# Rows of the last batch six schedule points later, and expert registers loaded in pairs

## The chip, the cores and the metric

The kernel runs on one NeuronCore of a Trainium2 chip. TensorE (PE, with weight loads shown apart as PEld) multiplies, VectorE (DVE) and ScalarE (ACT) work element by element, GpSimd (POOL) and SyncE (SP) mostly issue DMAs. The metric is device microseconds of one execution; lower is better. The time before is the median of three executions, 407.94 us (407.66 to 410.76).

## What is computed

Causal attention in blocks of 64 over 8 batches, 8 heads, 576 positions and head size 64, followed by a mixture of 8 experts with one expert for each token:

```python
scores = scale * q @ k.T, masked so that block_i >= block_j
attn   = softmax(scores);  x = attn @ v, laid out as rows of 512
logits = x @ w_gate                       # 8 experts
local  = sigmoid(x @ w_local)
e      = argmax(logits) if s == 0 or local < 0.5 else the expert of the row before
p      = softmax(logits)
out    = p[e] * (relu(x @ w1[e]) @ w2[e])    # 512 -> 1024 -> 512
```

There are 4,608 rows x. The expert of a row can depend on the row before it, so it is found by a scan along each batch.

## The kernel before

**Attention.** Two heads at a time make 32 steps, four to a batch. Through all of them PE is the busy engine. What the routing needs from a batch is worked into the steps of the next batches: `logits_of` and `tokens` find each row's expert, its factor and its rank among the rows of that expert; `rows_of_batch` turns a batch's result from columns into rows with PE transposes, VectorE divides them by the softmax sums, and a DMA stores them in `x_rows` in DRAM.

**Expert tiles.** Rows are then taken in tiles of 128 with one expert each. Phase 0 has 15 tiles made of rows of the first five batches; `slots_first` lists their rows. Phase 1 takes all that is left, the last batch included; `slots_second` lists its rows (`idx1`) and experts (`et1`). Twenty-three phase-1 tiles are always run, which makes 38 (tiles 0 to 37); five more stand behind a branch (L1469) that is not taken here. For a tile, GpSimd gathers its rows from `x_rows` (`gather`, L651), SyncE loads them transposed as `xT` (`rows_of`, L1388), VectorE copies the expert's first weights next to each other as `w1c` (`weights_of`, L1292), PE makes 32 products of 128 columns (`first_mm`, L1093), ScalarE applies the relu (L1096), PE makes 8 products of 512 columns (`second_mm`, L1330), ScalarE scales (L1335), and GpSimd scatters the rows to the output (L1338). In the loop the order on PE is `first_mm(i)`, `second_mm(i-1)`, `first_mm(i+1)`, and so on. `weights_of(i+1)` stands at the head of iteration i.

**Registers.** Which expert a tile has is known only on the chip. `expert` (L1102) reads the offset of its weights out of the table `et0` or `et1` in SBUF into a register on PE and into another on DVE (TENSOR_LOAD in the trace). DVE's is used by the `w1c` copy, PE's by `second_mm`.

**Work of the last batch.** When the first tiles run, the last batch is not done with. Two lists of steps remain, written as generators: `late()`, the chain that goes from the logits over `tokens` (its operations are L313 to L395) to `slots_second` (L563 to L629, and `experts_of`), and `rows()`, five steps that each turn 128 (the last 64) positions of the last batch into rows: four PE transposes (L720), one VectorE product (`x`, L767) and a DMA store. Calls of `point()` in the tile loop let them in: one after each half of `first_mm`, one before and one after `second_mm`, four to an iteration from i = 2 on, two in i = 1. At a point the chain goes first, if a credit in rough microseconds allows; where the chain takes nothing and at least `ROWS_AT` = 6 points have gone by since the last row step, a row step is let in. A chain step of kind "T" or "PE" has work for PE; a "T" step is held back until one point has gone by without work.

With the weights written in `late()`, the row steps before stand at points 7 (in `first_mm(3)`, between its halves), 13 (before `second_mm(3)`), 21 (before `second_mm(5)`), 30 (after `second_mm(7)`) and 38 (after `second_mm(9)`). The chain's transposes and products on PE stand at point 8 (`rta`, L330), 10 (`rtb`, L340), 12 (`rtd`, L350), 14 (`rtr`, L363), and 37, 42 and 44 (`rti`, L594).

**Stores and gathers.** A row step's store is held in a list and issued on SP one iteration later, behind that iteration's `rows_of` (or earlier, where `release()` is called). The first gather of phase 1, that of tile 15, is issued in iteration 12 ahead of `second_mm(11)`; before it, `release()` issues all that is still held, and the gather waits for the stores and for `idx1`. `rows_of(14)` comes on SP after that place.

Of the kernel before, what the change touches and what calls it, by code (L numbers as in the profile page):

```python
# [62 lines left out]
def kernel(  # L63
# [768 lines left out]
    with tc.tile_pool(name="atn_const", bufs=1) as cst, \  # L832
# [268 lines left out]
        def expert(ph, j, engines=(mybir.EngineType.PE, mybir.EngineType.DVE)):  # L1101
            return nc.values_load(  # L1102
                et_i[ph][0:1, j:j + 1], engines=engines, min_val=0,
                max_val=(E - 1) * WE,
                skip_runtime_bounds_check_because="the table is clamped to the last expert")
# [89 lines left out]
        for i in range(NPAIR):  # L1195
# [7 lines left out]
            if i == NPAIR - 1:  # L1203

                tiles = [(0, j) for j in range(NS[0])] + [(1, j) for j in range(NS[1])]
                ev = {j: expert(*tiles[j]) for j in range(2)}
# [79 lines left out]
    with ExitStack() as ffn:  # L1286
        f_p = ffn.enter_context(tc.tile_pool(name="ffn_s", bufs=2, reuse_waits="tile"))

        def weights_of(i):
            ev[i] = expert(*tiles[i])  # L1290
            w = f_p.tile([P, WE], BF16, tag="w1c%d" % (i % 2), name="w1c", bufs=1)
            ended["w"] = nc.vector.tensor_copy(w, w1_bf[:, bass.ds(ev[i], WE)])  # L1292
            return w

        f_p.tile([P, WE], BF16, tag="w1c1", name="w1c", bufs=1)
        f_p.tile([P, KO1, P], BF16, tag="xT0", name="xT", bufs=1)
        w_third = weights_of(2)
        for _ in range(2):
            steps.step()
# [46 lines left out]
        def late():  # L1346
            b = B - 1
            for weight, group in ((1.1, (lambda: half_batch(b, 1, gates=False),)),
                                  (1.5, (lambda: logits(b, 0), lambda: logits(b, 1)))):
                yield "PE" if weight < 1.2 else "T", weight  # L1350
                for out in [x() for x in group]:
                    out()
            yield "V", 0.4
            yield from tokens(*GROUPS[3], TS)
            yield "V", 0.8
            yield from slots_second(scratch_of([Sall.rearrange("p a h s -> p (a h s)")]))

        def rows():
            for t in range(NC):
                yield "PE", 0.7  # L1360
                if len(held) > 1:
                    release()
                rows_out(B - 1, t)()
# [9 lines left out]
            credit[0] -= spent  # L1373

        EACH, ROWS_AT = 0.6, 6
        credit, points = [0], [0]
        chain, others = Steps(late()), Steps(rows())
        def ps_x():
            return f_ps.tile([P, KO1, P], BF16, tag="rt", name="ps_x", bufs=3)
# [25 lines left out]
        more, tiles = tiles[-MORE:], tiles[:-MORE]  # L1405
# [24 lines left out]
        for i, (ph, j) in enumerate(tiles):  # L1430
            now, done = w, prev
            waiting = len(held)
            if i == 0:
                w = w_next
            elif i + 1 < len(tiles):
                w = w_third if i == 1 else weights_of(i + 1)
# [28 lines left out]
            if i == behind_tile:  # L1465

                nc.gpsimd.drain()
                n = nc.values_load(used[0:1, 0:1], min_val=0, max_val=E * BS)
                with tc.If(n > NS[1] - MORE, label="more"):  # L1469
                    more_tiles()  # L1470
        i = len(tiles) - 1
# [37 lines left out]
```

## Time and profile before

| | |
|---|---|
| median of three executions | 407.94 us |
| the profiled execution: time, span | 412.89 us, 410.8 us |
| mean granted PE clock | 0.991 |
| tile loop on PE, from `first_mm(0)` to the last product | 257.7 to 406.2 us of the span |
| DMA moved | 69.97 MB, mean 170 GB/s |

The profiled execution is 4.95 us above the median, 2.1 us of its time lie around the span, and times below are counted from the span's start. A row of the timeline gives start, length, engine, line, operation, the tiles written and read, the count of instructions merged, and in brackets how long the engine had been idle and what released it. Matmuls overlap by about 0.16 us at their ends, so a stretch is best measured from start to start.

### The profile page before, as it was taken

The page shows a single profiled execution, that of the slowest core. Times are in us where ns is not written, and L with a number is a line of the kernel's source. Part 1 is how long each engine was busy: PE and PEld are TensorE (multiplying, and loading weights), DVE is VectorE, ACT ScalarE, POOL GpSimd, SP SyncE. Part 2 cuts the span into 40 slices and gives each one's busy share as a digit, 9 for nine tenths or more (in the row PEclk, how much of TensorE's full clock was granted, in tenths as well). Part 3 has the DMA queues.
Part 4 walks back from the last instruction along what each step waited for, and adds up shares of the span by engine and source line. Part 5 has one row for each costly group of instructions (what it writes and reads, how often), then busy time and mean ns, then how long its engine had stood idle before and what let it go on. Part 6 is the DMA issues. An engine that isn't in the chain of part 4 may idle for free. (4 is left out here: it accounts for less than half of the span.)

```text
span 410.8 us, 14546 instructions
## 1 busy us (share of the span) xinstructions
PE 395.0 (96%) x5834; PEld 285.7 (70%) x5834; DVE 246.2 (60%) x505; ACT 225.7 (55%) x391; POOL 183.8 (45%) x250
## 2 busy tenths in 40 slices
PE   8999999999999999999998998979999999999985
PEld 7677777776776876776774666647777777777663
DVE  3444746646646677977999767877985333324220
ACT  4666666665765765665663654334444455445342
POOL 1325343144144054554351452246767676666603
PEclk9999999999999999999998999999999999999989
DMA  6579999998998999999978789853753544554521
GB/s 180 135 155 225 195 214 245 206 187 227 215 207 192 207 184 222 208 167 239 205 153 199 131 162 192 124 136 111 159 173 104 152 148 131 142 158 138 140 67 77
DMA packets 108819, 69.97 MB, mean 170 GB/s; under 512 B 74847, under 2 KB 100255, under 8 KB 108752
## 3 DMA queue, kind: packets, MB, share of 16 engines
q0 software_dynamic: 19200, 34.84, 40.6%
q1 hardware_dynamic: 89552, 34.19, 35.9%
q8 instruction: 48, 0.79, 0.8%
q14 instruction: 19, 0.16, 0.1%
HBM read 66.88 MB, written 14.70 MB: 199 GB/s over the span
## 5 line engine op out<-in xcount | busy, mean ns | idle before, releaser
L1019 DVE TENSOR_TENSOR S<-S,Pc 128x896 f32<-128x896 f32 (+2 forms) x96 | 86.4, 900 | 21.4 <-PE o L998 16.5
L977 PE MATMUL sc<-qkT 64*64 64x224 f32 (+6 forms) x1536 | 92.1, 369 | 0.7 <-DVE xg L818 0.7
L1292 DVE COPY w1c<-w_bf 128x4096 bf16 x36 | 44.2, 1235 | 58.5 <-PE ps_y L1330 26.1
L1096 ACT ACTIVATE hT<-ps_h 128x512 bf16<-128x512 f32 x76 | 44.1, 598 | 57.6 <-PE ps_h L1093 23.1
L1093 PEld LDWEIGHTS <-w1c 128*128 128x128 bf16 x1152 | 67.9, 98 | 10.9 <-issue 3.8
L977 PEld LDWEIGHTS sc<-qkT 64*64 64x64 f32 x1536 | 70.6, 135 | 3.2 <-DVE xg L818 1.1
L880 POOL COPY w_bf<-w_bf 128x512 f32<-128x512 f32 x61 | 42.8, 718 | 66.5 <-DMA w_bf<-in_k_dram 27.4
L1330 PE MATMUL ps_y<-w_bf,hT 128*128 x296 | 71.3, 383 | 1.0 <-issue 0.7
L1093 PE MATMUL ps_h<-xT,w1c 128*128 128x128 bf16 x1088 | 67.2, 220 | 2.6 <-ACTq L1469 2.1
L651 POOL DMA_INDIRECT xg<-x_rows,idx x38 | 49.7, 1309 | 42.2 <-issue 13.9
L987 ACT ACTIVATE Pc<-sc 128x448 f32<-128x448 f32 (+1 forms) x96 | 68.1, 716 | 0.0
L998 PE MATMUL o<-Pc,v 128*64 128x320 f32 (+2 forms) x512 | 57.6, 366 | 0.0
L1338 POOL DMA_INDIRECT out_dram<-y,idx x37 | 42.4, 1147 | 25.7 <-issue 9.5
L998 PEld LDWEIGHTS o<-Pc,v 128*64 128x64 f32 x512 | 35.0, 137 | 23.8
L987 ACT ACTIVATE S<-sc 128x576 f32<-128x576 f32 x64 | 42.0, 656 | 14.9 <-PE sc L977 14.6
L1330 PEld LDWEIGHTS <-hT 128*128 128x128 bf16 x296 | 27.7, 99 | 28.5 <-issue 3.1
L1011 ACT COPY oT<-o 128x576 f32<-128x576 f32 x32 | 20.5, 641 | 36.2 <-PE o L1007 36.2
L1335 ACT ACTIVATE y<-ps_y,xg 128x512 f32<-128x512 f32 x37 | 25.4, 687 | 20.7 <-PE ps_y L1330 17.1
L818 DVE TENSOR_TENSOR xg<-trx,rs 128x512 bf16<-128x512 f32 (+1 forms) x31 | 20.2, 684 | 26.2 <-PE trx L692 26.1
L998 PE MATMUL o<-S,v 128*64 128x320 f32 (+1 forms) x256 | 35.0, 392 | 0.3 <-ACT qkT L925 0.3
L1026 POOL MEMSET S<- 64x128 f32 x30 | 6.0, 200 | 63.2 <-DVE S L1021 22.5
L946 ACT COPY qkT<-kq 128x1024 f32<-128x1024 f32 x30 | 30.8, 1027 | 0.4 <-PE trx L692 0.4
(313 smaller groups left out, 442.3 us busy)
## 6 DMA issues: line engine op xcount, KB each, us to landing
w_bf<-in_moe_w_dram POOLq DMA_DIRECT2D x16, 1024.0 KB
w_bf<-in_k_dram SPq DMA_DIRECT2D x32, 256.0 KB
w_bf<-in_q_dram SPq DMA_DIRECT2D x32, 256.0 KB
v<-in_v_dram SPq DMA_DIRECT2D x64, 128.0 KB
x_rows<-xg POOLq DMA_DIRECT2D x24, 128.0 KB
qkl<-in_k_dram SPq DMA_DIRECT2D x32, 32.0 KB
qkl<-in_q_dram SPq DMA_DIRECT2D x32, 32.0 KB
vl<-in_v_dram SPq DMA_DIRECT2D x32, 32.0 KB
```

What stands on the lines that cost most here:

```text
L651: st = nc.gpsimd.indirect_dma_start(out=x, out_offset=None, in_=x_dram[:rows], in_offset=bass.IndirectOffsetOnAxis(ap=row_of(ph, j), axis= ...
L880: copies[j](m, raws[i][1 + j].rearrange("p h j d -> p j h d"))
L946: nc.scalar.copy(to.rearrange("p a (r s) -> p r a s", r=2), ps.rearrange("p r (a s) -> p r a s", a=2))
L977: nc.tensor.matmul(to[:, col + skip:col + n], lhsT=t[r, 0, k0:k0 + ST], rhs=t[r, 1, q0 + skip:q0 + n], start=True, stop=True)
L987: nc.scalar.activation(exps_at(i, c, q0, n, rows), ps[rows, :, col:col + n], func=AF.Exp, scale=scale_attn)
L998: nc.tensor.matmul(po[64 * h:64 * h + 64, VO + q0:VO + q0 + n], lhsT=vs[i][c][:, h, :], rhs=exps_at(i, c, q0, n, slice(0, P))[:, h, :], st ...
L1019: nc.vector.tensor_add(Ss[i][:, :, P * c:], Ss[i][:, :, P * c:], Pc[i % 2][:, :, POS[c]:POS[c] + n])
L1093: nc.tensor.matmul(ps[:, fo, :], lhsT=w[:, ko * F + f0:ko * F + f0 + P], rhs=xT[:, ko, :], start=(ko == 0), stop=(ko == KO1 - 1))
L1096: relu[0] = nc.scalar.activation(hT[:, half * (FO // 2):(half + 1) * (FO // 2), :], ps, func=AF.Relu)
L1292: ended["w"] = nc.vector.tensor_copy(w, w1_bf[:, bass.ds(ev[i], WE)])
L1330: nc.tensor.matmul(ps, lhsT=hT[:, fo, :], rhs=w2_bf[:, bass.ds(ev + fo * Dm, Dm)], start=(fo == 0), stop=(fo == FO - 1))
L1338: st = nc.gpsimd.indirect_dma_start(out=out_flat, out_offset=bass.IndirectOffsetOnAxis(ap=row_of(ph, j), axis=0), in_=y, in_offset=None, b ...
```

## The change

`weights_of(i)` loads the registers of tile i and of tile i + 1 when tile i's are not there yet, so the loads for tiles 2 and 3 stand together, then 4 and 5, and so on to 36 and 37; every second call loads nothing. The count of loads is the same. And the count of points since the last row step begins at -6 in place of 0, so the first row step waits for six points more.

```diff
         def weights_of(i):
-            ev[i] = expert(*tiles[i])
+            if i not in ev:
+                for n in range(i, min(i + 2, len(tiles))):
+                    ev[n] = expert(*tiles[n])
             w = f_p.tile([P, WE], BF16, tag="w1c%d" % (i % 2), name="w1c", bufs=1)
             ended["w"] = nc.vector.tensor_copy(w, w1_bf[:, bass.ds(ev[i], WE)])
             return w
...
         EACH, ROWS_AT = 0.6, 6
-        credit, points = [0], [0]
+        credit, points = [0], [-ROWS_AT]
         chain, others = Steps(late()), Steps(rows())
```

With the same weights, the row steps then stand at points 13, 21, 28 (after `first_mm(8)`), 35 (in `first_mm(10)`) and 43 (in `first_mm(12)`, between its halves). The chain keeps its order on each engine; a few of its steps move by one point, and `rta`, `rtb`, `rtd` and `rtr` stay where they were.

## The prediction

> **What bounds the kernel now.** I read the page's busy time by engine first, then PE's waits, and only then the timelines around the rows that the change moves.
>
> ```profile
> PE 395.0 (96%) x5834; PEld 285.7 (70%) x5834; DVE 246.2 (60%) x505; ACT 225.7 (55%) x391; POOL 183.8 (45%) x250
> ```
>
> PE is busy for 96% of the span. The PE part of the table of waits, first for 262 to 285 us, then for 282 to 388:
>
> ```profile
> PE rtb L340 <- DVE S L337: 1.3, 1, 1.3
> PE ps_y L1330 <- issue: 0.7, 2, 0.3
> ...
> PE ps_h L1093 <- issue: 0.3, 1, 0.3
> ```
>
> The columns are the sum, the count and the longest. After 282 us PE loses 0.3 us in all, so what the change does there counts only as work added to PE or as a wait that isn't there now. The one long wait before, `rtb`, is a step of the chain, and the first row step stands right ahead of it. PE's timeline there:
>
> ```profile
> 271.19 1.05 PE L1093 MATMUL ps_h<-S,w1c 128*128 128x128 bf16 x16
> 272.08 0.61 PE L720 MATMUL trx<-id_f,oT 128*128 128x128 f32 x4
> 272.52 1.06 PE L1093 MATMUL ps_h<-S,w1c 128*128 128x128 bf16 x16
> 273.93 0.27 PE L330 MATMUL rta<-id_f,S 128*5 128x128 f32 x1 [0.35 <-issue]
> 274.04 1.89 PE L1330 MATMUL ps_y<-w_bf,hT 128*128 x8
> 277.27 0.19 PE L340 MATMUL rtb<-S,ones_f 5*5 5x5 f32 x2 [1.34 <-DVE S L337]
> 277.61 1.95 PE L1093 MATMUL ps_h<-xT,w1c 128*128 128x128 bf16 x32 [0.16 <-PE rtb L340]
> ```
>
> And VectorE's in the same place:
>
> ```profile
> 268.43 1.23 DVE L1292 COPY w1c<-w_bf 128x4096 bf16 x1 [0.36 <-issue]
> 270.10 0.36 DVE L737 RECIPROCAL rs<-trl 128x32 f32<-128x32 f32 x1 [0.45 <-remote]
> ...
> 273.62 0.17 DVE L327 TENSOR_TENSOR S<-S 128x5 f32<-128x5 f32 x1
> 274.41 1.23 DVE L1292 COPY w1c<-w_bf 128x4096 bf16 x1 [0.62 <-issue]
> 275.55 0.68 DVE L767 TENSOR_TENSOR x<-trx,rs 128x512 bf16<-128x512 f32 x1
> 276.15 0.27 DVE L332 COPY S<-rta 5x128 f32<-5x128 f32 x1
> ```
>
> The reader is to see one chain: L327 ends at 273.79 and `rta` follows at 273.93; VectorE then copies `w1c`, makes row step 0's product, and only then does L332 and what follows up to L337, for which `rtb` and all of PE behind it wait. PE's four row transposes at 272.08 cost nothing here: without them `rta` would wait for L327 just as long.
>
> **The change part by part.** *(a) Row step 0 leaves this place.* On PE its 0.44 us (272.08 to 272.52) become idle time: 0. On VectorE its product goes out of the chain: 275.55 to 276.15, so `rtb` comes **0.60 us earlier**. Its store goes behind `rows_of(7)` on SP; nobody waits for that row until the gathers of phase 1.
>
> *(b) Loads in pairs.* All loads on PE, and two of them:
>
> ```profile
> L1102 PEldq TENSOR_LOAD <-et x38: 295/320/897, 249.0 to 393.8; - x38
> ...
> L1102 PEldq TENSOR_LOAD <-et x1: 300/300/300, 277.3 to 277.3; - x1
> ...
> L1102 PEldq TENSOR_LOAD <-et x1: 303/303/303, 310.5 to 310.5; - x1
> ```
>
> A load takes 0.30 us at the least, 0.32 in the middle; 38 remain. In the even part PE's own stream shows where one stands:
>
> ```profile
> 308.27 1.95 PE L1093 MATMUL ps_h<-xT,w1c 128*128 128x128 bf16 x32
> ...
> 310.25 1.89 PE L1330 MATMUL ps_y<-w_bf,hT 128*128 x8
> 311.98 1.95 PE L1093 MATMUL ps_h<-xT,w1c 128*128 128x128 bf16 x32
> ```
>
> The load at 310.5 belongs ahead of the products at 311.98: PE's sequencer is some 1.4 us early, and two loads in a row (0.6 us) fit under that; two of the longest on record (0.897, at the first tile) would stick out by 0.4. So in the even part the pairs cost and save nothing, and the eight products of 512 columns fill 310.25 to 311.98 without a gap in which a load could have cost. Without that cover a second load would cost 0.3 us and the next tile would have it back. In the chain it is another matter. The load at 277.3 stands between `rtb` and the next tile; it is tile 5's, which now comes with tile 4's: the 0.16 us wait at 277.61 goes, **-0.16**. Tile 4's call, just ahead of the `w1c` copy at 274.41, now makes two loads, on VectorE too: I take **+0.32** on the chain (between 0, if the second is hidden, and 0.62, the whole idle time that the row shows for the first). On PE the second load is ahead of the products at 271.19, and the idle time at `rta` (0.35, and 0.44 more from (a)) hides it. Tile 3's call at 268.43 makes no load: up to 0.36 less, but then L737 waits 0.45 for another reason, so I take half, **-0.18** (0 to -0.36).
>
> *(c) The row steps behind.* Steps 0 to 3 take places at or near those that steps 1 to 4 have now, so PE and VectorE do the same there. The fifth, at point 43 between the halves of the products at 308.27, is new, in a stretch in which PE never waits: **+0.44**, all of it (a lower bound would need a wait to hide it, and there is none).
>
> Sum: -0.60 - 0.16 + 0.32 - 0.18 + 0.44 = **-0.18 us**, with bounds -0.60 - 0.16 - 0.36 + 0.44 = -0.68 and -0.60 - 0.16 + 0.62 + 0.44 = +0.30. Against the profiled execution's own 412.89 us this gives 412.7; it stands 4.95 above the median of 407.94, and on that, 407.8.
>
> *(d) What the last row step sets late.* The first gather of phase 1 (tile 15) waits for every store of the last batch. Now the last is issued at 305.44, six microseconds ahead of that gather:
>
> ```profile
> 305.44 0.46 SPq L677 DMA_DIRECT2D x_rows<-x  x1
> 307.00:307.50 0.50, 0.50 (x4) 0.26 (x3) 0.50 (x2) 0.27 (x1) 0.00 (x0) 1.00 0.48 175
> 308.95 1.23 DVE L1292 COPY w1c<-w_bf 128x4096 bf16 x1 [0.27 <-issue]
> 311.60 1.38 POOL L651 DMA_INDIRECT xg<-x_rows,idx  x1 [0.56 <-DVE idx L432]
> 314.00:314.50 0.50, 0.50 (x4) 0.26 (x3) 0.50 (x1) 0.50 (x1) 0.32 (x1) 1.00 0.34 132
> L1388 SPq DMA_TRANSPOSE xT<-xg x1: 1200/1200/1200, 314.9 to 314.9; - x1
> 316.50:317.00 0.50, 0.50 (x13) 0.50 (x11) 0.00 (x0) 0.00 (x0) 0.49 (x1) 1.00 0.50 102
> 319.00 1.45 PE L1093 MATMUL ps_h<-xT,w1c 128*128 128x128 bf16 x23
> ```
>
> (The last two columns of the rows with two times are the DMA engines' share and GB/s.) The new step's product comes behind the `w1c` copy, which without its load ends at about 309.5: at 310.2, and the store is issued there. By the row of 305.44, whose bytes move until 307.5, its own move until 312.3; 0.4 us for the message (the gather's bytes end at 314.5, the transposing load starts at 314.9) gives 312.7. So the gather is 1.1 us late, the transposing load starts at 316.0, its bytes end at 318.1 (now 317.0, 2.1 after its start), and with 0.4 more tile 15 is ready at 318.5, for products at 319.00: hidden, by 0.5 us. `rows_of(14)` is now queued on SP behind that store; it starts near 310.7 and by the same 2.5 us is done at 313.2, two microseconds ahead of its tile. GpSimd's scatters behind the late gathers wait too, but their tiles `y` have three buffers, over 10 us of tile time.
>
> In a sentence of its own: the Trainium skill, "DMA: Bandwidth & Descriptors" (Anatomy of one DMA), puts a DMA at some 2.0 us plus its bytes over 436 GB/s, mostly for the receipt of the write, which for 64 KB is an estimate of 2.15 us and 312.4 in place of 312.7.
>
> **The rivals.** *Tile 15 waits (slower).* If the last store lands more than 1.6 us behind 311.60, PE stops ahead of 319.00. For it: the slack is the thinnest here. Against it: the 0.5 us above. The kernel's last output:
>
> ```profile
> 407.20 0.98 POOL L1320 DMA_INDIRECT out_dram<-y,idx  x1 [0.80 <-ACT y L1317]
> ```
>
> It is issued at 407.20, and the span ends at 410.8, 3.6 us later. If the row step's store took as long, it would land at 313.8, and PE would wait 0.6; with 0.4 us for the message 1.0: 408.8. At 1.6 us behind it decides the sign; for over 1% it would have to land after 317.3.
>
> *The clock falls (slower).* PE's idle time is moved about: more ahead of `rta`, less ahead of `rtb`. What a gap can cost is seen at the branch:
>
> ```profile
> 392.06 2.73 PE L1093 MATMUL ps_h<-xT,w1c 128*128 128x128 bf16 x32 [2.14 <-ACTq L1469]
> 393.00:394.00 1.00, 1.00 (x14) 1.00 (x11) 0.00 (x0) 0.60 (x1) 0.17 (x1) 0.51 0.28 107
> 394.79 2.60 PE ps_y L1330 x8
> 397.39 1.79 PE ps_h L1093 x32
> 399.18 1.73 PE ps_y L1330 x8
> ```
>
> After 2.14 us idle the granted clock was 0.51 in the next slice, and a tile took 2.73 + 2.60 in place of 1.79 + 1.73: 1.81 more, 409.6 here. Against it: the gaps to come are about 0.8 and 1.0 us, neither as long as the 1.34 of now.
>
> The Trainium skill, "TensorE: Matmul & The Clock Gate" (Part 1: The HAM clock gate), has the clock halved after an idle window of about 3.4 us that runs freely; by that rule no gap here would do it, but the trace's 2.14 us did, so the measurement decides and the chance isn't nil.
>
> *Late signals go away (faster).* Around 269 us several engines stand still at once: PE as below, and VectorE's L737 waits for something "remote" until 270.10.
>
> ```profile
> 268.11 0.80 PE L1330 MATMUL ps_y<-w_bf,hT 128*128 x2
> 269.25 0.38 PE L1330 MATMUL ps_y<-w_bf,hT 128*128 x1 [0.34 <-issue]
> 269.96 1.24 PE L1330 MATMUL ps_y<-w_bf,hT 128*128 x5 [0.33 <-issue]
> ```
>  These eight products take from 268.11 to 271.19, 3.08 us, where the same eight take 1.73 at 310.25. If loads cause it, one call fewer at 268.43 removes it: -1.35 beside the forecast, 406.4. Against it: the loads of the even part take as long and show no such gap.
>
> *Nothing happens.* The chain is held by something else than the product, and only (c) remains: +0.44 - 0.16, 408.2.
>
> **How the numbers follow.** About 1% (4 us) is what a measurement of this kernel can tell from no change. Forecast 0.66, its own range 407.2 to 408.3; tile 15 waits 0.13; the clock falls 0.04; late signals go 0.07; nothing 0.10. The time is 407.8. The range takes in the nothing and tile 15 cases and the low half of the faster one, with the 0.28 us by which two of the three executions before differ (407.66, 407.94): 406.6 to 409.2. No case reaches 4 us; what is left to both sides is 0.02 faster and 0.04 slower, and 0.94 lies within 1%.
>
> **What would show it.** Right: `rtb`'s wait near 1.0 in place of 1.34, none at the next tile, row transposes between the halves of the products at 308, every PE interval from 285 on as now but for that one, the gather of tile 15 near 312.7, and no wait at tile 15. Wrong: PE idle ahead of tile 15 or 14, a granted clock below 1 near 278, a gap at the pairs in the even part, or `rtb` as late as now.

## The result, and the profile after

| | time (us) | runs |
|---|---|---|
| before | 409.64 median (406.04 to 415.35) | 22 |
| after | 412.49 median (408.71 to 417.44) | 22 |
| after / before | 1.0064, 95% interval 1.0040 to 1.0088 | |

The change costs 0.64%, some 2.6 us (0.70% in the medians). The ratios leave out the executions of each kernel that are more than 1.5% above its fastest, which can by itself move a ratio by some 0.5%, so the table of the experiments gives the ratio of the medians of all executions as well. The prediction had 407.8 in a range of 406.6 to 409.2, level with before. The profiled execution of the changed kernel was one of its longest, 416.92 us with a span of 414.9; single executions of either kernel lie up to 9 us apart, so below the two are compared by the lengths of stages within a trace, and in time only over many runs. In the changed kernel, code behind the new lines has a line number two higher (L1330 is now L1332).

The page's first row after, and the waits of PE from 258 us to the end (sum, count, longest):

```profile
PE 396.2 (95%) x5834; PEld 287.9 (69%) x5834; DVE 245.2 (59%) x505; ACT 228.8 (55%) x391; POOL 185.5 (45%) x250
...
PE ps_h L1093 <- DMA xT<-xg: 2.3, 1, 2.3
PE ps_h L1093 <- PEq L1102: 1.5, 1, 1.5
PE rtb L340 <- DVE S L337: 0.9, 1, 0.9
PE rta L330 <- DVE S L327: 0.8, 1, 0.8
```

PE is as busy as before, to 1.2 us. Two waits of the chain are left, a long wait for a transposing load is new at the top, and at the branch PE now waits for its own register loads (PEq), 1.5 us where the wait for the branch was 2.1. First the chain, in VectorE's timeline and then in PE's:

```profile
275.90 0.16 DVE L327 TENSOR_TENSOR S<-S 128x5 f32<-128x5 f32 x1
276.78 1.23 DVE L1294 COPY w1c<-w_bf 128x4096 bf16 x1 [0.72 <-PE rta L330]
277.93 0.27 DVE L332 COPY S<-rta 5x128 f32<-5x128 f32 x1
...
276.12 0.27 PE L330 MATMUL rta<-id_f,S 128*5 128x128 f32 x1 [0.77 <-DVE S L327]
276.23 1.89 PE L1332 MATMUL ps_y<-w_bf,hT 128*128 x8
279.04 0.19 PE L340 MATMUL rtb<-S,ones_f 5*5 5x5 f32 x2 [0.93 <-DVE S L337]
279.16 1.96 PE L1093 MATMUL ps_h<-xT,w1c 128*128 128x128 bf16 x32
```

From the start of the `w1c` copy to `rtb` it is 2.26 us (279.04 - 276.78), where it was 2.86 (277.27 - 274.41): the row step's 0.60 is gone. The idle time ahead of the copy is 0.72 in place of 0.62 (0.33 in the further traces of before, see below), and the next tile's products follow `rtb` without a wait. From L327 to those products: 3.26 in place of 3.99.

Then the place of the last row step, in PE's timeline, and on to tile 15:

```profile
310.27 1.05 PE L1093 MATMUL ps_h<-xT,w1c 128*128 128x128 bf16 x16
311.16 0.60 PE L720 MATMUL trx<-id_f,oT 128*64 128x128 f32 x4
311.60 1.06 PE L1093 MATMUL ps_h<-xT,w1c 128*128 128x128 bf16 x16
...
314.41 1.95 PE L1093 MATMUL ps_h<-xT,w1c 128*128 128x128 bf16 x32
...
319.71 1.89 PE L1332 MATMUL ps_y<-w_bf,hT 128*128 x8
323.94 2.71 PE L1093 MATMUL ps_h<-xT,w1c 128*128 128x128 bf16 x32 [2.33 <-DMA xT<-xg]
326.44 2.82 PE L1332 MATMUL ps_y<-w_bf,hT 128*128 x8
329.10 1.95 PE L1093 MATMUL ps_h<-xT,w1c 128*128 128x128 bf16 x32
```

The row transposes stand between the halves; from tile 12's products to tile 13's it is 4.14 us (314.41 - 310.27) for 3.71 before. Three tiles on, PE stops for 2.33 us ahead of tile 15, and the tile behind the stop takes 5.16 us (329.10 - 323.94) where an undisturbed one takes 3.52 (1.79 + 1.73 in the prediction's rows behind the branch): its clock fell. The windows show it; the column ahead of the last two is the granted clock:

```profile
324.00:324.50 0.50, 0.50 (x11) 0.50 (x11) 0.00 (x0) 0.00 (x0) 0.31 (x1) 1.00 0.72 150
324.50:325.00 0.50, 0.50 (x12) 0.50 (x10) 0.00 (x0) 0.00 (x0) 0.50 (x1) 0.91 0.93 249
325.00:326.00 1.00, 1.00 (x12) 1.00 (x10) 0.00 (x0) 0.60 (x1) 0.69 (x2) 0.50 0.84 251
```

What tile 15 waited for, in the order of time over VectorE, SP and GpSimd, and the transposing loads begun between 318.5 and 321.5:

```profile
312.17 0.68 DVE L767 TENSOR_TENSOR x<-trx,rs 64x512 bf16<-64x512 f32 x1
312.87 0.46 SPq L677 DMA_DIRECT2D x_rows<-x  x1
313.58 0.19 DVE L432 SCALAR_TENSOR_TENSOR idx<-S 128x28 int32<-128x28 f32 x1
318.14 1.04 POOL L651 DMA_INDIRECT xg<-x_rows,idx  x1 [5.03 <-DVE w1c L1294]
...
L1390 SPq DMA_TRANSPOSE xT<-xg x1: 1191/1191/1191, 321.0 to 321.0; - x1
```

The row lists `idx` are ready at 313.77, and before, the gather followed 0.27 us behind them. Here it follows 4.4 us behind. The `w1c` copy named as releaser had ended at 316.14; of what the gather waits for, the last to come was the store, which was issued at 312.87. So the store took **5.27 us** from issue to the gather (318.14 - 312.87). From there it is 2.9 us to the transposing load and 2.9 to PE.

### The profile page after: what moved, and what is told of

Its sections match the earlier page's. It is cut to its first block, busy times and chain, and to the rows that moved or that the text cites. A ratio compares the mean times of both kernels' runs of the same rounds, so it can differ in the third digit from the quotient of the medians.

```text
span 414.9 us, 14544 instructions
## 1 busy us (share of the span) xinstructions
PE 396.2 (95%) x5834; PEld 287.9 (69%) x5834; DVE 245.2 (59%) x505; ACT 228.8 (55%) x391; POOL 185.5 (45%) x250
## 5 line engine op out<-in xcount | busy, mean ns | idle before, releaser
L1019 DVE TENSOR_TENSOR S<-S,Pc 128x896 f32<-128x896 f32 (+2 forms) x96 | 84.8, 883 | 24.3 <-PE o L998 17.6
L880 POOL COPY w_bf<-w_bf 128x512 f32<-128x512 f32 x61 | 45.9, 769 | 82.3 <-DMA w_bf<-in_k_dram 47.4
L1332 PE MATMUL ps_y<-w_bf,hT 128*128 x296 | 70.8, 383 | 0.0
L651 POOL DMA_INDIRECT xg<-x_rows,idx x38 | 48.6, 1279 | 42.1 <-ACT hT L1096 12.0
L1096 ACT ACTIVATE hT<-ps_h 128x512 bf16<-128x512 f32 x76 | 45.3, 597 | 30.7 <-PE ps_h L1093 29.0
L998 PEld LDWEIGHTS o<-Pc,v 128*64 128x64 f32 x512 | 36.6, 137 | 22.5
L1332 PEld LDWEIGHTS <-hT 128*128 128x128 bf16 x296 | 27.8, 99 | 26.9 <-issue 1.3
L998 PE MATMUL o<-S,v 128*64 128x192 f32 (+1 forms) x256 | 36.0, 392 | 1.5 <-DMA v<-in_v_dram 1.3
L714 ACT COPY LT<-trg 128x320 f32<-128x320 f32 x15 | 6.4, 426 | 46.7 <-PE trg L705 46.7
```

Source lines behind the costliest of these rows:

```text
L651: st = nc.gpsimd.indirect_dma_start(out=x, out_offset=None, in_=x_dram[:rows], in_offset=bass.IndirectOffsetOnAxis(ap=row_of(ph, j), axis= ...
L880: copies[j](m, raws[i][1 + j].rearrange("p h j d -> p j h d"))
L998: nc.tensor.matmul(po[64 * h:64 * h + 64, VO + q0:VO + q0 + n], lhsT=vs[i][c][:, h, :], rhs=exps_at(i, c, q0, n, slice(0, P))[:, h, :], st ...
L1019: nc.vector.tensor_add(Ss[i][:, :, P * c:], Ss[i][:, :, P * c:], Pc[i % 2][:, :, POS[c]:POS[c] + n])
L1096: relu[0] = nc.scalar.activation(hT[:, half * (FO // 2):(half + 1) * (FO // 2), :], ps, func=AF.Relu)
L1332: nc.tensor.matmul(ps, lhsT=hT[:, fo, :], rhs=w2_bf[:, bass.ds(ev + fo * Dm, Dm)], start=(fo == 0), stop=(fo == FO - 1))
```

## The experiments

Sixteen runs were made, each timed against before on the same chip (the third of before is one profiled execution, without a ratio). The table gives the ratio to before, with its 95% interval, then the ratio of the medians of all executions, and beside them two stages of the traced execution: the length from the start of tile 4's second products to tile 11's (the row steps' place), and from tile 13's to tile 15's (where tile 15 may wait; 7.03 us if it doesn't). They are differences of start times in PE's timeline.

| kernel | last store | ratio to before | of medians | tiles 4-11 | tiles 13-15 |
|---|---|---|---|---|---|
| before, first, second, third profile | early | - / 1.0041 (1.0006 to 1.0076) / - | - / 1.0004 / - | 26.55 / 26.56 / 26.56 | 7.49 / 7.60 / 8.34 |
| whole change | late | 1.0064 (1.0040 to 1.0088) | 1.0070 | 27.43 | 11.18 |
| whole change, again | late | 1.0098 (1.0064 to 1.0133) | 1.0102 | 27.00 | 8.27 |
| whole change, third | late | 1.0103 (1.0032 to 1.0173) | 1.0050 | 27.22 | 9.62 |
| rows only, twice | late | 1.0030 (0.9990 to 1.0071); 1.0084 (1.0046 to 1.0123) | 1.0011; 1.0046 | 27.22; 27.22 | 8.92; 11.60 |
| only the last step late | late | 1.0025 (0.9993 to 1.0058) | 0.9997 | 26.55 | 8.56 |
| whole, scatter behind | late | 1.0116 (1.0065 to 1.0167) | 1.0097 | 27.33 | 10.23 |
| whole, load ahead | late | 1.0075 (1.0033 to 1.0117) | 1.0130 | 27.39 | 8.36 |
| pairs only, twice | early | 1.0016 (0.9975 to 1.0057); 1.0018 (0.9975 to 1.0062) | 1.0010; 0.9993 | 26.85; 26.99 | 7.03; 8.35 |
| rows, last early, no pairs, twice | early | 1.0021 (0.9990 to 1.0052); 0.9995 (0.9940 to 1.0049) | 1.0020; 0.9971 | 27.01; 27.38 | 7.03; 8.26 |
| whole, last step early, twice | early | 1.0050 (1.0012 to 1.0089); 1.0063 (1.0025 to 1.0100) | 1.0015; 1.0063 | 27.59; 27.64 | 7.03; 8.68 |
| same, pairs from tile 3 on | early | 1.0099 (1.0055 to 1.0143) | 1.0083 | 28.15 | 8.38 |

**One part alone.** Rows only:

```diff
-        credit, points = [0], [0]
+        credit, points = [0], [-ROWS_AT]
```

> Only the row steps are six points later; registers are loaded one at a time as before. Theory S (the last row step's store lands some 5.3 us after it is issued, the gather of tile 15 waits for it, and PE stands still ahead of tile 15): the gather starts about 5 us after the store's issue, PE waits 2 to 3 us at tile 15, and the time is 2 to 3 us above before (0.5 to 0.8%). Theory P (the paired loads cost the time): within 0.5 us of before, no wait at tile 15.

Pairs only:

```diff
-            ev[i] = expert(*tiles[i])
+            if i not in ev:
+                for n in range(i, min(i + 2, len(tiles))):
+                    ev[n] = expert(*tiles[n])
```

> Only the loads are paired; the row steps stand as before. Theory S: within 0.5 us of before (0.16 us less at the next tile behind rtb, up to 0.3 us more on the chain), no wait at tile 15. Theory P: 2 to 3 us above before, with gaps on PE where pairs stand, every second tile.

The whole change, with the last row step one point behind the fourth (`given` counts the row steps):

```diff
-            if not spent and points[0] >= ROWS_AT and B - 1 in rs:
+            if not spent and points[0] >= (1 if given[0] == NC - 1 else ROWS_AT) and B - 1 in rs:
                 spent = others.point(credit[0])
                 points[0] = 0
+                given[0] += 1
```

> The whole change, but the last row step comes one point after the fourth, so its store is issued near 305 us, six microseconds ahead of the gather of tile 15. Theory S: the wait at tile 15 is gone, the chain's gain of some 0.6 us stays, and the time is 0 to 1 us below before. Theory P: 2 to 3 us above before, as the whole change.

The kernel before, with only its last row step put as late as the change puts it:

```diff
-            if not spent and points[0] >= ROWS_AT and B - 1 in rs:
+            if not spent and points[0] >= (ROWS_AT + 7 if given[0] == NC - 1 else ROWS_AT) and B - 1 in rs:
```

> Before, but the last row step stands behind the chain's end (its product about 0.7 us after idx), the other four as before, loads one at a time. Theory S: the store is issued near 312.0, lands near 317.3, tile 15 is ready near 323.1 and PE waits some 4 us (319.0 as before), with 1.6 us more where the clock falls after it: 4 to 6 us above before (1.0 to 1.4%). Theory P, or a cost of VectorE's order: within 0.5 us of before.

The first traces separate them. PE waits 1.7 us at tile 15 with rows only and 1.4 with only the last step late; it does not wait there with pairs only or with the last step early. (Second traces of the last two lose 1.3 and 1.7 us in that stage after all; more of this below.) Rows only, in GpSimd's and PE's timelines (its store was issued at 311.45):

```profile
316.62 1.04 POOL L651 DMA_INDIRECT xg<-x_rows,idx  x1 [4.93 <-DVE w1c L1292]
...
321.99 1.95 PE L1093 MATMUL ps_h<-xT,w1c 128*128 128x128 bf16 x32 [1.73 <-DMA xT<-xg]
```

Only the last step late, in SP's, GpSimd's and PE's:

```profile
310.97 0.46 SPq L677 DMA_DIRECT2D x_rows<-x  x1
314.62 1.30 POOL L651 DMA_INDIRECT xg<-x_rows,idx  x1 [4.83 <-DMA x_rows<-x]
...
320.35 1.95 PE L1093 MATMUL ps_h<-xT,w1c 128*128 128x128 bf16 x32 [1.38 <-DMA xT<-xg]
```

Here the trace itself names the store as what the gather waited for, and with it moved alone the wait is there. With the last step early the stores go out at 305.06 and the gather follows the row lists at once:

```profile
305.06 1.44 SPq L677 DMA_DIRECT2D x_rows<-x  x2
...
314.15 1.81 POOL L651 DMA_INDIRECT xg<-x_rows,idx  x1 [1.41 <-DVE idx L432]
```

The size of the wait was missed: I expected 4 us with only the last step late and it was 1.4, because this store took 3.65 us to the gather where that of rows only took 5.17. And in time the four kernels could not be told apart: 1.0016 to 1.0050, and of the two kernels without the wait one is the lowest and the other the highest.

**What makes the store slow.** The scatter of tile 10's rows is issued 1.7 us ahead of the store, and the transposing load of tile 14 right behind it. Each was moved away in the whole change:

```diff
-            st = nc.gpsimd.indirect_dma_start(
+            def scatter():
+                st = nc.gpsimd.indirect_dma_start(
...
+            if (ph, j) == HOLD:
+                kept.append(scatter)
+            else:
+                scatter()
...
+        kept, HOLD = [], tiles[10]
...
                 gathers(i + AHEAD, relu[0] if i > NS[0] + 1 else None)
+                for x in kept:
+                    x()
+                kept.clear()
```
```diff
+            if i == 12:
+                rows_of(i + 2)
             if i:
...
-            if i + 2 >= AHEAD:
+            if i + 2 >= AHEAD and i != 12:
                 rows_of(i + 2)
```

> The whole change, with the scatter of tile 10 issued behind the gathers of tiles 15 and 16 instead of ahead of them. Theory 'the store's completion stands behind the scatter's writes': without that scatter the gather of tile 15 goes out about 3.6 us behind the issue of the last row step's store, as in the run with only the last step late (3.65), in place of 5.27; PE's wait at tile 15 falls from 2.3 to about 0.7 us. Rival 'the store needs 5 us wherever it stands, or is slowed by the transposing load behind it': the gather still goes out 5.0 to 5.3 us behind the store, and the wait stays at 1.7 to 2.3. Times: 1 to 2 us below the whole change by the first, level with it by the second.

> The whole change, with the transposing load of tile 14 put on SP's queue ahead of the last row step's store, not behind it. Theory 'the transposing load, begun 0.5 us behind the store, slows the store's completion': the load's bytes have moved before the store is issued, and the gather of tile 15 goes out 3.6 us or less behind the store; wait at tile 15 at most 0.7. Theory 'it is the scatter': the gather still goes out about 5 us behind the store, and PE waits 1.7 to 2.3 at tile 15.

> The whole change once more, on one chip with the three others, so that they are compared with it and not only with before. Theory 'the late store': PE waits 1.5 to 2.5 us at tile 15 again, the gather goes out about 5 us behind the store, and the time is 1 to 4 us above before, more where the granted clock falls behind the wait. Rival 'the first measurement was mostly scatter between runs': the time is within 0.5 us of before.

The whole change beside them had a store that was quicker by itself, in SP's timeline, the DMA issues (the last figure is the time to landing) and GpSimd's:

```profile
309.46 0.46 SPq L677 DMA_DIRECT2D x_rows<-x  x1
...
x_rows<-x SPq DMA_DIRECT2D x1, 64.0 KB, 2.8
...
313.13 1.38 POOL L651 DMA_INDIRECT xg<-x_rows,idx  x1 [3.42 <-DVE w1c L1294]
```

3.67 us from issue to gather, 0.9 of it behind the landing that the profile gives. So one trace of an edit says little here. With the load ahead it was 3.58 (313.17 to 316.75), and PE waited 1.2 us at tile 15, where the whole change beside it waited 1.1. With the scatter behind it was 3.17, but what comes next took longer:

```profile
307.99 0.46 SPq L677 DMA_DIRECT2D x_rows<-x  x1
311.16 1.71 POOL L651 DMA_INDIRECT xg<-x_rows,idx  x1 [6.81 <-DMA xT<-xg]
314.51 1.02 POOL L1341 DMA_INDIRECT out_dram<-y,idx  x1 [0.30 <-issue]
...
320.07 1.95 PE L1093 MATMUL ps_h<-xT,w1c 128*128 128x128 bf16 x32 [3.04 <-DMA xT<-xg]
```

From the gather to tile 15's products it now is 8.9 us (320.07 - 311.16) for 5.8 in the whole change's first trace, and PE waits 3.04. That the moved scatter did this is not shown: the same way took 8.5 us in two traces in which no scatter was moved and the store was early (the third of before and the pairs from tile 3 on, both below). Neither theory is shown either: over all late stores the time from issue to gather was 3.17, 3.58, 3.65, 3.67, 3.67, 5.17, 5.25 and 5.27 us, and the same kernel has both 3.67 and 5.27. Why it falls now on the one and now on the other stays open.

**A version without the loss, and before against itself.** Rows later and the last one early, with single loads (the first and third edits above together):

> Row steps six points later, the last of them one point behind the fourth, and registers loaded one at a time as before. If the pairs bring nothing and the late store is the only harm: no wait at tile 15, rta's and rtb's waits as in the run of the row steps alone (1.3 and 0.5, and 0.16 at the next tile), and a tile loop within 0.5 us of that with the whole change and the last step early (136.7 us from the first to the last start of second products); time within 1 us of before.

> The kernel before, as a kernel of its own beside its own runs. It tells how much of the small ratios so far (1.002 to 1.005) is the measurement: 1.000 with an interval that holds it, if nothing is. Its second profile tells which parts of the first were accidents. Theory 'the 1.35 us at 269 and the granted clock's fall behind the branch were of that one execution': this one's tile loop, from the first to the last start of second products, is near 136.5 us instead of 140.0, with a gap of 1.1 us at the branch. Rival 'they belong to the kernel before': again near 140.

> A third profile of the kernel before, for the same question: tile loop near 136.5 us or near 140, the gap at the branch 1.1 or 2.1 us, and the start of the first second products, which so far stands between 260.5 and 266.5 us in kernels whose work up to there is the same.

The first had no wait at tile 15, a tile loop (from tile 0's second products to tile 36's) of 135.4 us, and 1.0021: level with before, not faster. Its second trace (its run is among the last four) had a loop of 141.6 us, with 1.2 us lost at tile 15 and, at the branch, a gap of 2.27 us with slow products behind it; so 135.4 is not what the version always takes. Before against itself gave 1.0041, though the medians differ by 0.0004, so a ratio of 0.4% alone shows nothing here, whatever its interval. Its further profiles have loops of 139.06 and 140.44 us, near the first one's 139.99, so the length was no accident, as I had thought. One part of it was: the eight products that took 3.08 us from 268.11 in the first take 1.89 and 1.87 in the others. The second profile's row at the branch, then the third's waits:

```profile
390.96 1.95 PE L1093 MATMUL ps_h<-xT,w1c 128*128 128x128 bf16 x32 [1.59 <-ACTq L1469]
...
PE ps_h L1093 <- ACTq L1469: 2.1, 1, 2.1
PE ps_h L1093 <- DMA xT<-xg: 1.1, 1, 1.1
```

The gap at the branch is 1.6 and 2.1 us (behind the longer one the products took 3.10 us for 1.95), and in the third profile tile 15 waits 1.1 us with an early store: from the gather to the products it took 8.5 us that time (317.33 - 308.84). The slack of tile 15 was thin in the kernel before.

**Do the pairs cost something where nothing covers them?** With pairs from tile 2 on, two loads stand right behind the branch, on PE's path. With pairs from tile 3 on, none stands there:

```diff
-                for n in range(i, min(i + 2, len(tiles))):
+                for n in range(i, min(i + 1 + (i > 2), len(tiles))):
```

> The whole change with the last row step one point behind the fourth, once more, on one chip with the next kernel. No wait at tile 15, 1.4 to 1.6 us at the branch behind the pair of loads there. Theory 'the pairs cost at the branch, where nothing covers a second load': 0.4 us above the kernel with single loads and the last step early, so 1.000 to 1.004 of before. Rival 'it is 0.5% slower for a reason that the trace hasn't shown': 1.004 or more again.

> The same, with the pairs shifted by one tile: tile 2's registers are loaded alone, then 3 and 4, 5 and 6, and so on, so that no load stands right behind the branch. Theory 'the pairs cost only where nothing covers them': the gap at the branch falls from 1.4 to 1.6 to 1.1 us or less, no 0.36 us gap two tiles ahead of it, and the tile loop is 0.4 to 0.8 us shorter than that of the kernel with the pairs from tile 2 on (136.7): about 136.0. Rival 'pairs cost as such, wherever they stand': the loop stays at 136.7 or above.

The gap at the branch was 1.1 us with the shift, and 1.4 and 1.2 in the two traces without it. But the loop with the shift was 139.5 us, not the 136.0 expected, and without it 136.7 and then 139.0. The shifted kernel lost elsewhere: 28.15 us in tiles 4 to 11, with a wait of 1.0 us for VectorE's L611 that no other trace has, and 8.38 in tiles 13 to 15, though its store is early. The kernel without the shift lost there too in its second trace (8.68), where I had expected no wait. Both measured as slow as the whole change. Where the pairs do show is a short gap ahead of a tile's products. In the whole change's first trace two loads end right where the products start, and in its second a gap of 0.36 us stands two tiles ahead of the branch, where the branch's own register is loaded as well:

```profile
L1102 PEldq TENSOR_LOAD <-et x2: 302/304/306, 298.1 to 298.5; - x2
298.84 1.95 PE L1093 MATMUL ps_h<-xT,w1c 128*128 128x128 bf16 x32 [0.26 <-PE ps_y L1332]
```

And in the second trace:

```profile
383.16 1.95 PE L1093 MATMUL ps_h<-xT,w1c 128*128 128x128 bf16 x32 [0.36 <-PE ps_y L1332]
...
391.97 1.95 PE L1093 MATMUL ps_h<-xT,w1c 128*128 128x128 bf16 x32 [1.63 <-PEq L1102]
```

**Late store or pairs.** Since kernels with pairs and an early store had measured slow, both parts ran again on one chip:

> Pairs alone, once more, beside rows alone and the whole change on one chip. Theory 'the pairs carry the loss': 2 to 3 us above before in the mean of the runs, as every kernel so far that has pairs and the later rows. Theory 'the late store and its wait at tile 15 carry it': within 1 us of before, no wait at tile 15. Rival 'the loss is in the spread between loadings of a program': a mean that differs from this kernel's first one (0.4 above before) by as much as the whole change differs from before (2.6).

> Rows alone, once more. Theory 'the late store': a wait of 1.1 to 2.3 us at tile 15, and 1.5 to 3 us above before. Theory 'the pairs': the same wait in the trace, but within 1 us of before, as in its first measurement (0.6), since the rows' 0.6 us at rtb and the shorter gap at the branch (1.1 us, where all three profiles of before have 1.6 to 2.1) pay for most of it.

> Rows six points later, the last one early, no pairs, once more. Both theories expect the least time of the four: between 1 us below and 0.5 us above before, no wait at tile 15 or one of at most 1.1 (as the third profile of before has one), tile loop 135.4 to 137.5.

> The whole change, third measurement, for the same comparison on one chip. If the loss is of the kernel and not of one chip or one loading: 2 to 3.5 us above before again. Its profile gives a third sample of the store's time to the gather (5.3 and 3.7 so far), of the wait at tile 15 (2.3 and 1.1) and of the stage ahead of the tile loop (263.3 and 265.5 to the first second products; before has 260.5 to 262.5).

Pairs alone came out level again (1.0018), rows with the last one early level (0.9995), rows with the late store slower (1.0084), and the whole change like those (1.0103). The medians of all executions put the four kernels in the same order, closer together: before 415.2, pairs alone 414.9, rows with the last one early 414.0, rows with the late store 417.1, the whole change 417.3. Rows only, the second trace (its store was issued at 310.55):

```profile
315.80 1.04 POOL L651 DMA_INDIRECT xg<-x_rows,idx  x1 [5.00 <-DMA xT<-xg]
...
322.33 1.95 PE L1093 MATMUL ps_h<-xT,w1c 128*128 128x128 bf16 x32 [2.97 <-DMA xT<-xg]
```

Rows only and the version with the last one early differ in the place of one row step alone. In tiles 13 to 15 that is 3.3 us in these two traces (11.60 and 8.26), and 1.9 in the first two (8.92 and 7.03). Over all traces that stage is 9.6 us in the mean of eight with a late store, and 7.8 in the mean of ten with an early one, a difference of **1.8 us** with a standard error of 0.5. The two sets overlap (8.3 to 11.6, and 7.0 to 8.7): seven of the ten early ones lose 0.5 to 1.7 us there too, as the pairs from tile 3 on do, whose gather was issued at 312.00:

```profile
320.51 1.95 PE L1093 MATMUL ps_h<-xT,w1c 128*128 128x128 bf16 x32 [1.19 <-DMA xT<-xg]
```

So in the traces the late store costs time at tile 15. That it carries the measured loss is not shown: with the last step alone put late there is a wait of 1.4 us, and the time is 1.0025, or 0.9997 in the medians. Pairs alone cost nothing that can be measured. What isn't explained is that pairs and later rows together, with an early store, measured 1.0050, 1.0063 and 1.0099, while each of them alone is level; the traces show 27.6 to 28.2 us in tiles 4 to 11 for 26.55, which is 1.0 to 1.6 us of it. Of this 0.44 is the row step that moved into the stage, and for the rest no cause is shown.

## Why the prediction was wrong

- **(a) Row step 0, -0.60: right.** 2.86 became 2.26 us.
- **(b) Pairs in the chain: right.** The wait at the next tile is gone. The second load at tile 4's call shows as only 0.10 us of idle time more beside the first trace of before, but that trace was unusual: ahead of the same copy its two others, and all five further traces with single loads, have 0.33. With two loads there it is 0.70 to 0.77 in seven of nine traces (0.96 and 1.00 in the others), some 0.4 more, where I took 0.32. Here are the third trace of before, then the whole change's second, with its two loads:

```profile
271.42 1.23 DVE L1292 COPY w1c<-w_bf 128x4096 bf16 x1 [0.33 <-issue]
...
273.91 1.23 DVE L1294 COPY w1c<-w_bf 128x4096 bf16 x1 [0.71 <-PE rta L330]
...
L1102 DVEq TENSOR_LOAD <-et x2: 301/307/313, 273.0 to 273.4; - x2
```

  Together with (a) the stretch from L327 to the next tile, 3.26 us, is 0.73, 0.70 and 0.43 shorter than in the three traces of before, where these terms had -0.44. Tile 3's copy does start without idle time now; whether the -0.18 taken for it reaches the chain, the traces do not separate.
- **(b) Pairs in the even part, 0: partly wrong.** I had said that a second load costs 0.3 us where its cover is gone, and did not look for such places. PE waited 0.26 us at 298.84 in the first trace and 0.36 at 383.16 in the second, and at the branch the loads are now what PE waits for, though not longer than before (1.5, 1.6 and 2.3 us, for 2.1, 1.6 and 2.1). In time the pairs alone are level.
- **(c) The fifth row step, +0.44: right.** 3.71 became 4.14 us.
- **(d) The last store, hidden by 0.5 us: this is the step that failed.** I had it land 2.5 us behind its issue, from the row of 305.44, by the end of its bytes plus 0.4 us. But by the time the gather asks for that store it has long been done, so the row does not show when. Eight late stores took 3.2 to 5.3 us to the gather, and PE, forecast to wait for nothing, waited 2.3, 1.1 and 1.7 us at tile 15 in the three traces of the whole change. The way behind, from the gather to tile 15's products, I had at 5.8 us (312.7 to 318.5); in the traces where PE waited it was 5.4 to 8.9. With 2.5 + 5.8 I was 0.5 us ahead of the products; with 3.67 + 6.27 (second trace) they wait 1.1, and with 5.27 + 5.80 (first) 2.3. The transposing load of tile 14, queued behind the store, was in time, as predicted.
- **The rival "tile 15 waits"** is what happened, and its condition (more than 1.6 us behind 311.60) was the right one. Its price of 1.0 us was drawn from the kernel's last output, 3.6 us, which is the shorter of the two times seen; it fits the second trace (3.67, and a wait of 1.1) and is too small for the first (5.27, and 2.3). The Trainium skill, "DMA: Bandwidth & Descriptors" (Anatomy of one DMA), gave an estimate of 2.15 us for 64 KB, with a fit that it states for DMAs issued from GpSimd, while this store is issued from SP. By these runs the estimate is short by 1 to 3 us to the point at which the waiting gather goes out.
- **The rival "the clock falls"** came on top in the first trace, in another place: behind the 2.33 us gap the granted clock was 0.50, and the tile took 1.64 us more, near the 1.81 that I had worked out from the branch. Behind the gap of 1.1 in the second trace, tile 15's products took 1.95 us, as undisturbed ones do.
- **The rival "late signals go away"** was about one execution, not about the kernel. The eight products that took 3.08 us from 268.11 take 1.9 in the two further traces of before and 1.7 to 2.1 in those of the whole change; with single loads it came once more (2.84, rows only, second trace).
- **The baseline.** 407.94 was the median of three; 409.64 is that of 22. The profiled execution of before had, at the branch, a gap and a fall of the clock that the second profile has only in part (8.77 us over the two tiles there, for 10.98) and the third in full (10.88), so what the change does there could not be read from one trace.

Does this account for the loss? Three traces to a side give these means, in us, between starts of second products on PE:

| stage | before | whole change | difference |
|---|---|---|---|
| start of the span to tile 0's | 261.24 | 263.26 | +2.0 |
| tile 0's to 4's (the chain) | 20.64 | 19.67 | -1.0 |
| tile 4's to 13's (row steps) | 33.58 | 34.33 | +0.8 |
| tile 13's to 15's (the late store) | 7.81 | 9.69 | +1.9 |
| tile 15's to the last (the branch is here) | 77.80 | 76.56 | -1.2 |
| to the end of the span | 8.40 | 8.40 | 0.0 |

Inside the tile loop the late store is the largest loss, but the other stages give most of it back, and the loop as a whole is 0.4 us longer. Two of the gains need care: the chain's holds the 1.35 us of one execution, and the branch's holds falls of the clock that two of the three traces of before have. The larger part of the difference in span, 2.0 of 2.4 us, lies ahead of tile 0's second products, where the change does next to nothing; the single values are 260.5 to 262.5 and 261.0 to 265.5, so three traces to a side do not tell whether that is chance. Measured were 2.6 us with 22 runs to a side, and 4.0 and 4.3 in two smaller comparisons (0.98 and 1.03%; in the medians 4.2 and 2.1). So the step that failed is known, and its wait is seen in every trace of the whole change; what makes up the measured time is open.

## What to carry to other kernels

- A store's end is shown only where something waits for it. Take the time from issue to use from a row with a waiter (3.6 us at the last output here), not from the end of its bytes, and put the spread of such rows into the range: a slack of half a microsecond at the end of a chain of three DMAs is no slack.
- When a list of side work is moved later as a whole, ask of its last member alone who waits for it. Here four of five row steps could move without a loss that could be measured, and moving the fifth by itself made a wait.
- Measure the kernel against itself before reading anything into half a per cent.

## What the runs showed of the hardware

- The same store, in the same place of the same program, took 3.67 us to its gather in two executions and 5.27 in a third. The eight late stores fall into two groups, 3.2 to 3.7 and 5.2 to 5.3, with none between.
- From the issue of a gather to the products that use its rows, through the transposing load, it took 5.4 to 8.9 us in the ten traces in which PE waited for that load at tile 15; a waiting chain of two DMAs has a spread of 3.5 us here.
- One register load ahead of a VectorE copy shows as 0.33 us of idle time, two in a row as 0.70 to 0.77 in seven traces of nine.
- The length of a gap alone does not decide whether PE's clock falls. Behind gaps of 2.14 us (before, at the branch) and 2.33 (after, at tile 15) the granted clock was 0.51 and 0.50. Behind 3.04 us (scatter behind) it was 1.00 and the products took 1.95 us, as undisturbed ones do, and so they did behind the longest wait at the branch, in the whole change's third trace:

```profile
394.11 1.95 PE L1093 MATMUL ps_h<-xT,w1c 128*128 128x128 bf16 x32 [2.34 <-PEq L1102]
```

- The work ahead of the tile loop, which the change hardly touches, took from 259.7 to 269.4 us to the first second products, over all traces. In several of the long ones PE waits for loads of `v`, here in the first trace of rows only:

```profile
PE o L998 <- DMA v<-in_v_dram: 3.5, 4, 1.5
```

  That spread is larger than anything the change does, and no run here tells what it comes from.
